# First unit of a retention and softplus FFN kernel: attention in chunk runs at five slots, and a new order of the weight conversions

## The chip, the cores and the metric

One core of one Trainium2 chip runs the whole program. The metric is device time in microseconds, the median of three runs. Five engines matter: PE (TensorE), DVE (VectorE), ACT (ScalarE), POOL (GpSimd) and SP, which issues all transfers. Each works through its own instructions in program order, and semaphores tie them together.

## The reference

Eight sequences of 576 tokens with eight heads of 64 go through a retention layer (scores times a decay matrix, no softmax). Its output, 4608 rows of 512, goes through a feed-forward layer with softplus between two products.

```python
scores = scale * np.matmul(q, k.transpose(0, 1, 3, 2))
Dmat = np.where(rel >= 0, gamma[:, None, None] ** rel[None, :, :], 0.0)
x = np.matmul(scores * Dmat, v)          # then heads side by side: (4608, 512)
...
h = x @ w_in                             # 512 -> 2048
g = np.maximum(h, 0.0) + np.log1p(np.exp(-np.abs(h)))
return g @ w_out                         # 2048 -> 512
```

The weights arrive as float64. The kernel makes float32 values of them on the chip, and splits every factor of the big products into a head and a rest, so that each product is three matmuls.

## The kernel before, in words

**Units and chunks.** The 4608 tokens are nine units of 512; a unit is four chunks of 128 tokens. The attention of a chunk is two steps (`m`), one for each half of the heads, so steps 2c and 2c+1 belong to chunk c. A step has scores (`scores_mm`, into `S`), sums for the running state (`sums_mm`, into `T`), and, once the scores are masked (`a`, DVE) and the states are there (`u` and `s` on DVE, `sx` and the decay of `s` on POOL), values and cross products (`values_mm`, `cross_mm`, into `O`). All of these are products of 64 x 64 tiles, four of which fill the array.

**The opening** (about the first 23 us) does chunks 0 to 3, the tokens of unit 0, with whole-tile forms, and converts the first weight pieces.

**The first unit** is the loop `for i in range(NF)` of 16 slots, and this is where the change lies. Slot i computes a block of `h` for unit 0 (12 matmuls, `hidden_mm`), its softplus (ACT: Abs, Exp, Ln; DVE: `softplus`; ACT: head `softplus_split`; DVE: rest `softplus_rest`), and the output product `y` of slot i-1 (12 matmuls, `output_some`). So `y` of slot i stands on PE behind `h` of slot i+1, and begins with the rest of `g`. Beside it each slot converts two weight pieces, one of w_in (`win`) and one of w_out (`wout`). A piece takes five steps: `weight_p` (ACT), `weight_t` (DVE), `weight_b` (DVE, needs p and t), `weight_c` (ACT, the head), `weight_d` (DVE, the rest). `weight_dl` is d, then the load of the piece five further on into the freed buffer `wst`, then for `win` the store to `split`. Meanwhile the attention of chunks 4 to 8 is needed for unit 1: every odd slot runs one step's scores and sums and the values of the step before, as three single runs on PE ahead of `h`.

**After it** come `plain_slot` calls, where a whole chunk is done in one run by `chunk_products(steps, done)`: scores and sums of a chunk, values and cross products of the chunk before it, interleaved by row groups of the array. In that run a one-element memset on POOL (`mark`) stands between the first sums and the second ones, since both row groups write one bank. The first such run, ahead of the first plain slot, takes the half chunk left over by the single steps; the second has one done step instead of two.

POOL scales the values of a step as soon as they are loaded (`scale_values`), decays the states, and makes the rest of the attention output `xt` (`half_x`).

Of the kernel before, what the change touches and what calls it, by code (L numbers as in the profile page):

```python
# [19 lines left out]
P = 128  # L20
# [20 lines left out]
START_WEIGHTS = 3  # L41
OPENING = 3
NOPEN = AHEAD + 2
# [3 lines left out]
NPIECE = 2 * NF  # L47
NJ = NF // 2
OPEN1 = 6
# [20 lines left out]
LAST = 320  # L70

# [13 lines left out]
def retention_softplus_ffn(ctx: ExitStack, tc, first, whole, others, consts, w, out):  # L85
# [6 lines left out]
    const, att, moe = pool("const", 1), pool("att", 2), pool("moe", 2)  # L92
    rawp, xpool, wpool = pool("rawp", 2), pool("xpool", 1), pool("wpool", 1)
# [8 lines left out]
    later = {}  # L102
# [47 lines left out]
    def load_rest(m):  # L150
        place = later["odd"] if m >= 2 * CHUNKS - 1 and m % 2 else rawp
# [7 lines left out]
    def load_step(m):  # L159

        if m == 0:
            at = 0
            for x in parts:
                nc.sync.dma_start(x, first[:, at:at + x.shape[1]])
                at += x.shape[1]
            k, q = parts[0][:, 0:2 * C], parts[0][:, 2 * C:4 * C]
            kp, v = parts[1][:, 0:2 * C], parts[1][:, 2 * C:4 * C]
        else:
            if m < NOPEN:
                place = openp if m < OPEN1 else openp2  # L170
                r = place.tile([P, 8 * C if m < FIRST else RAW], F32, name=f"raw{m}")
# [152 lines left out]
    def chunk_products(steps, done):  # L324
# [18 lines left out]
        for n in range(max(len(x) for x in pairs)):  # L343
            if n == 2 * len(steps) and sums_of(steps, 0):
                mark = nc.gpsimd.memset(later["mark"].tile([1, 1], F32, tag="mark", name="mark"), 0.0)
# [134 lines left out]
    def logs(h):  # L480

        ab = moe.tile([P, T], F32, tag="ab", name="ab", bufs=ABUFS)
        nc.scalar.activation(ab, h, AF.Abs)
        nc.scalar.activation(ab, ab, AF.Exp, scale=-1.0)
        nc.scalar.activation(ab, ab, AF.Ln, bias=1.0)
        return ab

# [73 lines left out]
    def load_weight(n):  # L561
        if n < NPIECE:
            wl[n] = wst.tile([P, PIECE, 2], I32, tag="wst", name="wst", bufs=WBUFS)
            nc.sync.dma_start(wl[n].rearrange("p c a -> p (c a)"), w[n // 2, n % 2])
# [24 lines left out]
    def weight_dst(n):  # L589
        p = n // 2  # L590
        if n % 2:
            return wouts[p][:, HI], wouts[p][:, LO]
# [13 lines left out]
    def weight_store(n):  # L606
        if n < NPIECE and n % 2 == 0:
            nc.sync.dma_start(split[n // 2].bitcast(F32), wins[n // 2].bitcast(F32))
# [88 lines left out]
    first_a, first_b = {3: 0, 5: 1, 6: 2}, {4: 0, 6: 1}  # L697
# [22 lines left out]
    def next_scores(m):  # L720
        new = ps_open.tile([P, 2, T], F32, tag="pair", name="pair")
        if m < FIRST:
            scores_whole(m, new)
        else:
            scores(m, new)
        return new
# [4 lines left out]
    for m in range(AHEAD):  # L731
        if m < FIRST:
            bank = (ps_att if m % 2 else ps_val).tile([P, 2, T], F32, tag="bank" if m % 2 else "val", name="bank")
            sums_whole(m, bank)
            values_whole(m, bank)
            if m == 0:
                next_scores(1)
            if m + 2 < AHEAD:
                new = next_scores(m + 2)
            ready = live[m]  # L740
            if m < FIRST - 1:
                state_whole(m, ready)
            if m == 0:
                scale_values(1)
            if m + 2 < AHEAD:
                scale_values(m + 2)
            parts_out = values_out(m, nc.gpsimd if m < FIRST - 1 else nc.vector)
            if m == 0:
                masked_whole(1)
            if m + 2 < FIRST:  # L750
                masked_whole(m + 2)
            if m == FIRST - 1:
                weight_b(2)
            parts_out()
            if m == FIRST - 1:
                weight_c(2)
            if m == FIRST - 1:
                scale_values(AHEAD)
                state_whole(m, ready)
        else:  # L760
            sums(m, new)
            scores_out(m)
            states_out(m)
        if m in first_a:
            weight_a(first_a[m])
        if m in first_b:
            weight_b(first_b[m])
            weight_c(first_b[m])
        if m == 5:
            weight_dl(0)  # L770
        if m == AHEAD - 1:
            weight_d(2)
        if m == AHEAD - 2:
            load_step(AHEAD + 1)
    weight_dl(1)
    load_weight(WBUFS + 2)
    weight_store(2)
# [5 lines left out]
    constant[0] = constants(consts_sb[:, 0:SMALL], consts_sb[:, SMALL:])  # L783


    for i in range(NF):
        n = START_WEIGHTS + 2 * i
        m = AHEAD + (i - 1) // 2
        step = i % 2
        if step:  # L790
            bank = ps_att.tile([P, 2, T], F32, tag="bank", name="bank")
            scores(m, bank)
            sums(m, bank)
            values(m - 1, bank)
# [5 lines left out]
        if i == 1:  # L800
            weight_dl(n - 1)
        weight_b(n)
        if i:
            weight_t(n + 1)
        h = hidden_mm(i, i % 2)
        ab = logs(h)
        if i > 1:
            weight_dl(n - 1)
        if i < NF - 1:
            softplus(h, ab)  # L810
        if i == 0:
            weight_t(n + 1)
        if step:
            _, t, cols = place(m - 1)
            where = (B11, B21)[(m - 1) % 2], STAGE[(m - 1) % 2, t], cols
            halves_out(m - 1)
            scores_out(m)
            states_out(m)
            if i < NF - 1:
                scale_values(m + 1)  # L820
            if m == NOPEN:
                open_pools.close()
                place_weights(ctx.enter_context(tc.tile_pool(name="wpool2", bufs=1)), NF)
        if i == NF - 1:
            softplus(h, ab)
        weight_c(n)
        if not step:
            weight_dl(n)
        gs[0, i] = softplus_split(ab)
        softplus_rest(gs[0, i], ab)  # L830
        if step:
            weight_dl(n)
            half_x(*where, nc.gpsimd)
        weight_p(n + 1)
        weight_b(n + 1)
        if n + 2 >= NPIECE and "ring" not in later:
            weight_pools.close()
            for name, bufs in (("ring", RING), ("odd", 2)):
                later[name] = ctx.enter_context(tc.tile_pool(name=name + "2", bufs=bufs))
            load_step(2 * CHUNKS - 1)  # L840
            scale_values(2 * CHUNKS - 1)
# [8 lines left out]
    for name, bufs in (("quad", QUADS), ("mark", 2), ("sum", 1)):  # L850
        later[name] = ctx.enter_context(tc.tile_pool(name=name + "2", bufs=bufs, side="right"))
    two = later["two"] = ps_att.tile([P, 2, T], F32, tag="bank", name="two")
# [4 lines left out]
    groups = [([m + 1], [m])]  # L857
    for ch in range(m // 2 + 1, NCHUNK + 1):
        groups.append(([2 * ch, 2 * ch + 1] if ch < NCHUNK else [], [k for k in (2 * ch - 2, 2 * ch - 1) if k > m]))
    groups = groups[::-1]  # L860

    def next_steps(steps):
        ks = [k for m in steps for k in ((m + 1, m + 2) if len(steps) == 1 else (m + 2,)) if k < NSTEP]
# [11 lines left out]

    def values_taken(steps, done):
        if steps:
            scores_out(*steps)
        if done:
            halves_out(*done)  # L880

    def group_out(steps, done):
        values_taken(steps, done)
        if steps:
            states_out(*steps)
# [12 lines left out]
    def plain_slot(u, p, xa, xb, rest, group=None, blocks=(), jobs=(), starts=()):  # L898
# [3 lines left out]
        ahead = u == 1 and p == 0  # L902
        if ahead:
            chunk_products(*group)
            coming_steps = next_steps(group[0])
# [7 lines left out]
        if ahead:  # L913
            group_out(*group)
        elif group:
# [5 lines left out]
        if group and not ahead:  # L921
# [78 lines left out]
    def store_out(j):  # L1000
# [3 lines left out]
        (0, prepare, PLAIN + 1), (0, prepare_whole, PLAIN), (0, prepare_sums, PLAIN), (1, prepare_split, PLAIN),  # L1004
# [450 lines left out]
```

## Time and profile before

| | |
|---|---|
| median of 3 runs | 817.8 us (817.5 to 818.37) |
| profiled execution, span | 815.8 us |
| PE busy | 808.2 us (99%) |
| DVE, ACT, POOL busy | 560.6, 389.2, 123.7 us |
| moved by DMA | 211.75 MB, mean 260 GB/s |
| granted TensorE clock | 0.9 or more in all 40 slices |

The profiled execution is 2.0 us shorter than the median, which counts what lies around the span. The page gives busy times, the chain of work that ended last (from the last instruction back to what released each step), and groups of instructions by line. TensorE's busy share alone says little here, since its instruction ends are modelled; the chain tells where it waited.

### The profile page before, as it was taken

How to read it: one execution, taken by the hardware profiler on the slowest of the kernel's cores; microseconds unless marked ns; L12 is line 12 of the kernel's file. 1: busy time of each engine (PE TensorE's matmuls, PEld its weight loads, DVE VectorE, ACT ScalarE, POOL GpSimd, SP SyncE). 2: the span in 40 equal slices, each digit the busy share in tenths (PEclk: the TensorE clock that was granted, in tenths of full speed). 3: DMA queues.
4: the chain of work that ended last, by engine and by line, in shares of the span. 5: the costliest groups of instructions: out<-in, count | busy, mean ns of one | idle time of the engine just before them, and what ended most of it. 6: DMA issues, size and time to landing. Idle time of an engine off the chain costs nothing.

```text
span 815.8 us, 18681 instructions
## 1 busy us (share of the span) xinstructions
PE 808.2 (99%) x7322; PEld 666.2 (82%) x7322; DVE 560.6 (69%) x953; ACT 389.2 (48%) x681; POOL 123.7 (15%) x223
## 2 busy tenths in 40 slices
PE   8999999999999999999999999999999999999998
PEld 6788888888888888888888888888888888888886
DVE  5999976777666774867669974555679944335785
ACT  6888863334323244434344554324355734434553
POOL 4322321320321420112122001112100000000000
PEclk9999999999999999999999999999999999999999
DMA  9998979989899882798987777878657776666674
GB/s 359 324 318 292 313 239 389 334 312 324 264 311 359 304 315 79 239 330 271 310 286 236 220 229 244 261 235 264 215 177 217 221 246 193 196 191 194 194 221 159
DMA packets 149847, 211.75 MB, mean 260 GB/s; under 512 B 10880, under 2 KB 114816, under 8 KB 149760
## 3 DMA queue, kind: packets, MB, share of 16 engines
q1 hardware_dynamic: 149760, 210.56, 78.3%
q8 instruction: 59, 0.97, 0.5%
q14 instruction: 28, 0.23, 0.1%
HBM read 168.05 MB, written 42.47 MB: 258 GB/s over the span
## 4 chain that ended last, share of the span: by engine, by line
PE 95%; DMA 2%; DVE 2%; ACT 0%; issue 0%; SPq 0%; DVEq 0%
PE acc L892 22%; PE sum L1183 20%; PE y L518 16%; PE two L892 14%; PE h L475 5%; PE two L1183 4%; PE third L892 3%; PE third L211 2%; PE third L1183 2%; PE acc L1183 2%; PE two L195 2%; PE two L299 2%; PE two L311 1%; DMA raw<-others 1%; DMA raw<-whole 1%; DVE wst L587 0%
## 5 line engine op out<-in xcount | busy, mean ns | idle before, releaser
L892 PE MATMUL acc<-xt,ring 128*128 128x512 f32 x780 | 196.4, 389 | 0.1
L892 PEld LDWEIGHTS acc<-xt,ring 128*128 128x128 f32 x780 | 146.3, 188 | 30.9 <-issue 0.3
L1183 PE MATMUL sum<-parts,ring 128*128 128x512 f32 x708 | 170.9, 392 | 0.0
L1183 PEld LDWEIGHTS sum<-parts,ring 128*128 128x128 f32 x708 | 131.6, 188 | 27.8
L1177 DVE TENSOR_TENSOR parts<-g,parts 128x512 fp32r<-128x512 f32 x168 | 115.4, 694 | 45.0 <-ACT parts L1173 42.3
L518 PE MATMUL y<-wout,g 128*128 128x512 f32 x564 | 137.2, 392 | 0.3 <-DVE g L497 0.3
L1173 ACT CAST parts<-g 128x512 fp32r<-128x512 f32 x168 | 103.9, 622 | 67.6 <-DVE parts L1177 27.3
L518 PEld LDWEIGHTS y<-wout,g 128*128 128x128 f32 x564 | 104.8, 188 | 22.9 <-DVE g L497 0.7
L892 PE MATMUL two<-xt,ring 128*128 128x512 f32 x486 | 123.3, 389 | 0.0
L892 PEld LDWEIGHTS two<-xt,ring 128*128 128x128 f32 x486 | 91.2, 188 | 18.9
L1205 ACT ACTIVATE g<-g 128x512 f32<-128x512 f32 x72 | 45.3, 629 | 59.4 <-DVE g L1220 35.6
L188 POOL TENSOR_TENSOR qv<-qv,consts_sb 128x256 f32<-128x256 f32 x61 | 47.4, 778 | 164.7 <-DMA qv<-others 157.7
L1220 DVE TENSOR_TENSOR g<-two,g 128x512 f32<-128x512 f32 x24 | 16.6, 692 | 77.8 <-PE two L892 77.8
L1218 ACT COPY g<-acc 128x512 f32<-128x512 f32 x24 | 14.1, 588 | 77.6 <-PE acc L892 77.6
L497 DVE TENSOR_TENSOR g<-ab,g 128x512 fp32r<-128x512 f32 x42 | 32.3, 769 | 26.4 <-ACT g L493 25.7
L493 ACT CAST g<-ab 128x512 fp32r<-128x512 f32 x42 | 26.1, 621 | 46.2 <-PE y L518 41.5
L475 PE MATMUL h<-xt,win 128*128 128x512 f32 x192 | 47.4, 396 | 0.3 <-DVE win L604 0.3
L475 PEld LDWEIGHTS h<-xt,win 128*128 128x128 f32 x192 | 35.3, 188 | 8.2 <-DVE win L604 0.6
L1258 ACT ACTIVATE g<-acc 128x512 f32<-128x512 f32 x24 | 14.3, 598 | 49.3 <-PE acc L892 49.3
L211 PEld LDWEIGHTS third<-qv,keys 64*64 64x64 f32 x776 | 27.0, 134 | 8.9 <-issue 7.7
L253 DVE TENSOR_TENSOR a<-two,mask 128x512 f32<-128x512 f32 (+1 forms) x28 | 19.0, 679 | 22.2 <-PE third L211 15.2
L1183 PE MATMUL two<-parts,ring 128*128 128x512 f32 x144 | 33.6, 389 | 0.0
(177 smaller groups left out, 1190.4 us busy)
## 6 DMA issues: line engine op xcount, KB each, us to landing
ring<-split SPq DMA_DIRECT2D x121, 256.0 KB, 4.9
ring<-combined SPq DMA_DIRECT2D x108, 256.0 KB, 3.9
ring<-outcombined SPq DMA_DIRECT2D x96, 256.0 KB, 3.5
qv<-others SPq DMA_DIRECT2D x61, 320.0 KB, 5.5
ring<-outsplit SPq DMA_DIRECT2D x72, 256.0 KB, 3.8
wst<-w SPq DMA_DIRECT2D x32, 512.0 KB, 5.8
keys<-others SPq DMA_DIRECT2D x61, 256.0 KB, 5.4
split<-win SPq DMA_DIRECT2D x16, 512.0 KB, 6.7
```

What stands on the lines that cost most here:

```text
L188: nc.gpsimd.tensor_mul(v, v, f.unsqueeze(2).broadcast_to([P, 4, D]))
L211: mm = nc.tensor.matmul(L["T"][rows[h], t, part[s]], L["kp"][rows[t], s, rows[h]], L["v"][rows[t], s, rows[h]], start=True, stop=True, ski ...
L253: nc.vector.tensor_mul(a[:, :, at], src.rearrange("p h (s c) -> p h s c", c=HC), mask.unsqueeze(1).unsqueeze(1).broadcast_to([P, 2, 2 * le ...
L475: nc.tensor.matmul(h, wins[p][:, a, kt * P:(kt + 1) * P], xt[:, b, T1 + half, kt % 2], start=(n == 0), stop=(n == 3 * NKT - 1))
L493: nc.scalar.copy(g[:, HI], ab)
L497: nc.vector.tensor_sub(g[:, LO], ab, g[:, HI].bitcast(F32))
L518: nc.tensor.matmul(ys[u][tt], g[:, a, tt * P:(tt + 1) * P], wouts[p][:, b], start=(p == 0 and n == 0), stop=(p == NF - 1 and n == 2))
L892: nc.tensor.matmul(bank, w[:, ta, kt * P:(kt + 1) * P], xt[:, tb, x, kt], start=start and k == 0, stop=k == 5, skip_group_check=True)
L1173: nc.scalar.copy(t[:, HI], g_slot(J, n))
L1177: nc.vector.tensor_sub(t[:, LO], g_slot(J, n), t[:, HI].bitcast(F32))
L1183: nc.tensor.matmul(bank[m], w[:, a, m * P:(m + 1) * P], t[:, b], start=start and n == 0, stop=n == 2, skip_group_check=True)
L1205: nc.scalar.activation(c, c, AF.Softplus)
```

## The change

The attention of chunks 4 to 8 moves from single steps at the odd slots to whole-chunk runs at slots 1, 4, 8, 12 and 15 (`GROUPS`), placed on PE behind `h` of the slot rather than ahead of it. Step 8 leaves the opening. The run writes its sums to the other `h` bank (`third`). Steps 8 to 13 use four rotating buffers; loads and scalings are placed by tables (`LOADS`, `SCALES`). The weight pieces are converted in a new order (`PIECES`: win of slot i+1 ahead of wout of slot i), with the five steps of a piece at new places between the softplus steps. The run ahead of the first plain slot is gone, the one two slots later is a whole one, and the last `y` of the unit comes ahead of the first plain slot.

```diff
-START_WEIGHTS = 3
-NOPEN = AHEAD + 2
+STEPS1 = 14
+PIECES = [(0, 0)] + [x for i in range(NF - 1) for x in ((i + 1, 0), (i, 1))] + [(NF - 1, 1)]
-OPEN1 = 6
+OPEN1 = 7
...
+GROUPS = {1: (4, None), 4: (5, 4), 8: (6, 5), 12: (7, 6), 15: (8, 7)}
+ODD = 12
+LOADS = {4: (12, 13), 8: (14, 15), 12: (16, 17), 15: (18, 19)}
+SCALES = {2: (10, 11), 7: (12, 13), 11: (14, 15), 14: (16, 17)}
...
-        if m >= AHEAD:
+        if m >= FIRST:
             nc.gpsimd.tensor_mul(v, v, f.unsqueeze(2).broadcast_to([P, 4, D]))
...
-    first_a, first_b = {3: 0, 5: 1, 6: 2}, {4: 0, 6: 1}
+    first_a, first_b = {3: 0, 5: 1, 6: 2}, {4: 0, 6: 1, 7: 2}
...
-    for m in range(AHEAD):
+    for m in range(FIRST):
...
     for i in range(NF):
-        n = START_WEIGHTS + 2 * i
-        m = AHEAD + (i - 1) // 2
-        step = i % 2
-        if step:
-            bank = ps_att.tile([P, 2, T], F32, tag="bank", name="bank")
-            scores(m, bank)
-            sums(m, bank)
-            values(m - 1, bank)
-            if i < NF - 1 and m + 1 >= NOPEN:
-                load_step(m + 1)
-        weight_p(n)
-        weight_t(n)
-        weight_c(n - 1)
...
+        near, out_now, far, out_next = 2 * i + 1, min(2 * i + 2, NPIECE - 1), 2 * i + 3, 2 * i + 4
...
+        group = [chunk_steps(ch) for ch in GROUPS.get(i, ())]
         h = hidden_mm(i, i % 2)
-        ab = logs(h)
...
+        if group:
+            later["third"] = ps_h.tile([P, T], F32, tag=f"h{(i + 1) % 2}", name="third")
+            chunk_products(*group)
...
+            for k in LOADS.get(i, ()):
+                load_step(k)
+        ab = moe.tile([P, T], F32, tag="ab", name="ab", bufs=ABUFS)
+        nc.scalar.activation(ab, h, AF.Abs)
+        weight_dl(near)
+        weight_t(far)
+        weight_c(out_now)
+        weight_dl(out_now)
+        weight_t(out_next)
+        nc.scalar.activation(ab, ab, AF.Exp, scale=-1.0)
+        weight_p(far)
+        if group:
+            states_out(*group[0])
+        weight_b(far)
+        nc.scalar.activation(ab, ab, AF.Ln, bias=1.0)
+        weight_p(out_next)
+        softplus(h, ab)
+        weight_b(out_next)
         gs[0, i] = softplus_split(ab)
         softplus_rest(gs[0, i], ab)
+        weight_c(far)
+        if group:
+            values_taken(*group)
+            for m in group[1]:
+                _, t, cols = place(m)
+                half_x((B11, B21)[m % 2], STAGE[m % 2, t], cols, nc.gpsimd)
+        for k in SCALES.get(i, ()):
+            scale_values(k)
...
+    output_some(CPU)
     for p in range(2 * PLAIN):
-        group = groups.pop() if p % 2 == 0 else None
+        group = groups.pop() if p and p % 2 == 0 else None
```

On PE a slot pair before is `h`, `y`, then a step as three runs with a new `bank`, then the next `h`; L195 are scores, L211 sums, L299 values, L311 cross products. Slot 5 of before:

```order
L518 MATMUL y_668<-wout_182,g 128x512 x3
L195 MATMUL bank<-qv,keys 64x64 x8
L211 MATMUL bank<-qv,keys 64x64 x8
L299 MATMUL bank<-a,raw_530 64x64 x8
L311 MATMUL bank<-raw_530,s 64x64
...
L311 MATMUL bank<-raw_530,u 64x64
L475 MATMUL h<-xt,win_828 128x512 x12
```

The chunk run of slot 4 in the changed kernel, its middle and its end; L203 are scores, L307 values, L319 cross products, L219 sums:

```order
L203 MATMUL two<-raw 64x64
L307 MATMUL two<-a,raw 64x64
...
L307 MATMUL two<-a,raw 64x64 x9
L319 MATMUL two<-raw,s 64x64
L219 MATMUL third<-raw 64x64
...
L319 MATMUL two<-raw,sx 64x64
L219 MATMUL third<-raw 64x64
L518 MATMUL y_657<-wout_185,g 128x512 x3
```

The attention now stands between `h` and `y`, at fewer places, and its sums go to `third`, the bank of the next `h`.

On ACT, L483 to L485 (before) and L801, L807, L812 (changed) are Abs, Exp and Ln, L574 is `weight_p`, L599 `weight_c`, L493 the head of `g`. A slot before:

```order
L483 ACTIVATE ab<-h 128x512
L484 ACTIVATE ab<-ab 128x512
L485 ACTIVATE ab<-ab 128x512
L599 CAST wout_184<-wst 128x512
L493 CAST g<-ab 128x512
L574 ACTIVATE wst<-wst 128x512 x2
L599 CAST win_914<-wst 128x512
```

The same in the changed kernel:

```order
L801 ACTIVATE ab<-h 128x512
L599 CAST wout_187<-wst 128x512
L807 ACTIVATE ab<-ab 128x512
L574 ACTIVATE wst<-wst 128x512
L812 ACTIVATE ab<-ab 128x512
L574 ACTIVATE wst<-wst 128x512
L493 CAST g<-ab 128x512
L599 CAST win_935<-wst 128x512
```

A weight step now stands between each two softplus steps, and Ln comes two instructions later.

On POOL, L452 is the rest of `xt`, L196 the scaling of a step's values, L282 and L289 the copies of `sx`, L301 the decay of `s`. Around the run of slot 8 the changed kernel has:

```order
L353 MEMSET mark 1x8
L282 COPY sx<-s 64x256
L289 COPY sx<-u 64x256
L301 TENSOR_TENSOR s<-s,consts_sb 128x256
L452 TENSOR_TENSOR xt<-xs,xt 128x2x128 x2
L196 TENSOR_TENSOR qv<-qv,consts_sb 128x256 x2
L353 MEMSET mark 1x8
```

Before, each odd slot had one `xt` and one scaling; now two and two follow each other directly behind a run, with nothing between them on POOL.

## Rows read from the trace of the kernel before

**Rows 1.** Page, part 1, and two stretches (length, engine busy, clock, DMA share, GB/s)

```profile
PE 808.2 (99%) x7322; PEld 666.2 (82%) x7322; DVE 560.6 (69%) x953; ACT 389.2 (48%) x681; POOL 123.7 (15%) x223
...
20.00:40.00 20.00, 18.74 (x218) 14.57 (x213) 18.96 (x36) 16.28 (x32) 7.87 (x12) 1.00 0.95 337
40.00:60.00 20.00, 20.00 (x146) 16.42 (x147) 18.29 (x35) 17.11 (x30) 4.46 (x8) 1.00 0.90 306
```

**Rows 2.** Chain, 48 to 53 us: start, length, engine, tile, line, count

```profile
48.48 2.72 PE y L518 x12
51.20 0.39 PE bank L195 x16
...
52.29 2.95 PE h L475 x12
```

**Rows 3.** Chain, from the end of the first unit to the third chunk run

```profile
118.95 0.07 issue
...
120.17 2.96 PE acc L892 x12
...
134.02 0.20 PE third L211
...
135.57 2.95 PE y L518 x12
...
159.82 0.20 PE third L211
...
161.84 2.95 PE y L518 x12
```

**Rows 4.** PE in order of time: start, length, line, tile, in brackets idle before

```profile
20.88 0.46 PE L195 MATMUL pair<-raw 64*64 64x64 f32 x16 [0.64 <-DMA raw<-others]
...
22.90 3.01 PE L475 MATMUL h<-xt,win 128*128 128x512 f32 x12
...
26.77 3.03 PE L475 MATMUL h<-xt,win 128*128 128x512 f32 x12
...
35.55 3.02 PE L518 MATMUL y<-wout,g 128*128 128x512 f32 x12 [0.28 <-DVE g L497]
...
40.00 3.04 PE L475 MATMUL h<-xt,win 128*128 128x512 f32 x12 [0.35 <-DVE win L604]
```

**Rows 5.** DVE in order of time, end of the opening and slots 3 to 4

```profile
23.80 0.87 DVE L417 TENSOR_TENSOR xt<-x,xt 128x256 fp32r<-128x256 f32 x1
...
25.32 0.68 DVE L604 TENSOR_TENSOR win<-wst,win 128x512 fp32r<-128x512 f32 x1
25.92 0.78 DVE L604 TENSOR_TENSOR wout<-wst,wout 128x512 fp32r<-128x512 f32 x1
...
49.50 0.92 DVE L587 SCALAR_TENSOR_TENSOR wst<-wst 128x512 int32<-128x512 int32 x1
50.34 0.96 DVE L581 TENSOR_SCALAR wst<-wst 128x512 int32<-128x512 uint32 x1
```

**Rows 6.** ACT in order of time, the softplus of slot 3

```profile
43.14 0.60 ACT L483 ACTIVATE ab<-h 128x512 f32<-128x512 f32 x1
43.77 0.64 ACT L484 ACTIVATE ab<-ab 128x512 f32<-128x512 f32 x1
44.44 0.63 ACT L485 ACTIVATE ab<-ab 128x512 f32<-128x512 f32 x1
44.98 0.64 ACT L599 CAST wout<-wst 128x512 fp32r<-128x512 f32 x1
```

**Rows 7.** POOL in order of time, end of the opening and slots 3 to 4

```profile
23.77 0.62 POOL L188 TENSOR_TENSOR raw<-raw,part 128x256 f32<-128x256 f32 x1 [0.55 <-DMA raw<-others]
...
49.03 0.84 POOL L188 TENSOR_TENSOR qv<-qv,consts_sb 128x256 f32<-128x256 f32 x1 [1.12 <-DMA qv<-others]
49.83 1.19 POOL L444 TENSOR_TENSOR xt<-xs,xt 128x256 fp32r<-128x256 f32 x1
```

**Rows 8.** Tile wst, from the issue of a load to its landing

```profile
DMA to landing us min/median/max: 3.5/5.8/11.4
```

More of the change, by code (lines that the diff above doesn't have):

```diff
@@ L150, in load_rest @@
     def load_rest(m):
-        place = later["odd"] if m >= 2 * CHUNKS - 1 and m % 2 else rawp
+        place = rawp if m // 2 % 2 else later["odd"]
         qv = place.tile([P, RAW - KEYS], F32, tag="qv", name="qv")
@@ L606, in weight_store @@
     def weight_store(n):
-        if n < NPIECE and n % 2 == 0:
-            nc.sync.dma_start(split[n // 2].bitcast(F32), wins[n // 2].bitcast(F32))
+        p, second = PIECES[n]
+        if not second:
+            nc.sync.dma_start(split[p].bitcast(F32), wins[p].bitcast(F32))
     def weight_dl(n):
@@ L720, in next_scores @@
     def next_scores(m):
[L721 to L726, printed above, removed]
+        scores_whole(m, ps_open.tile([P, 2, T], F32, tag="pair", name="pair"))
     next_scores(0)
@@ L730, in retention_softplus_ffn @@
     masked_whole(0)
-    for m in range(AHEAD):
[L732 to L763, printed above, removed]
+    for m in range(FIRST):
+        bank = (ps_att if m % 2 else ps_val).tile([P, 2, T], F32, tag="bank" if m % 2 else "val", name="bank")
+        sums_whole(m, bank)
+        values_whole(m, bank)
+        if m == 0:
+            next_scores(1)
+        if m + 2 < FIRST:
+            next_scores(m + 2)
+        ready = live[m]
+        if m < FIRST - 1:
+            state_whole(m, ready)
+        if m == 0:
+            scale_values(1)
+        if m + 2 < AHEAD:
+            scale_values(m + 2)
+        parts_out = values_out(m, nc.gpsimd if m < FIRST - 1 else nc.vector)
+        if m == 0:
+            masked_whole(1)
+        if m + 2 < FIRST:
+            masked_whole(m + 2)
+        parts_out()
+        if m == FIRST - 1:
+            scale_values(AHEAD)
+            state_whole(m, ready)
         if m in first_a:
@@ new lines, in retention_softplus_ffn, with values_taken, group_out, chunk_steps @@
+    place_weights(ctx.enter_context(tc.tile_pool(name="wpool2", bufs=1)), NF)
+    two = later["two"] = ps_att.tile([P, 2, T], F32, tag="bank", name="two")
+    load_step(AHEAD + 2)
+    def values_taken(steps, done):
+        if steps:
+            scores_out(*steps)
+        if done:
+            halves_out(*done)
+    def group_out(steps, done):
+        values_taken(steps, done)
+        if steps:
+            states_out(*steps)
+    def chunk_steps(ch):
+        return [] if ch is None else [2 * ch, 2 * ch + 1]
@@ L837, in retention_softplus_ffn @@
+        if i >= NF - 2 and "ring" not in later:
             weight_pools.close()
[L838 to L841, printed above, removed]
+            later["ring"] = ctx.enter_context(tc.tile_pool(name="ring2", bufs=RING))
             for _ in range(RING):
@@ L849, in retention_softplus_ffn @@
     piece_pools.close()
-    for name, bufs in (("quad", QUADS), ("mark", 2), ("sum", 1)):
+    for name, bufs in (("quad", QUADS), ("sum", 1)):
         later[name] = ctx.enter_context(tc.tile_pool(name=name + "2", bufs=bufs, side="right"))
-    two = later["two"] = ps_att.tile([P, 2, T], F32, tag="bank", name="two")
     acc = ps_h.tile([P, T], F32, tag="h0", name="acc")
     later["third"] = ps_h.tile([P, T], F32, tag="h1", name="third")
-    groups = [([m + 1], [m])]
-    for ch in range(m // 2 + 1, NCHUNK + 1):
-        groups.append(([2 * ch, 2 * ch + 1] if ch < NCHUNK else [], [k for k in (2 * ch - 2, 2 * ch - 1) if k > m]))
+    groups = [(chunk_steps(ch) if ch < NCHUNK else [], chunk_steps(ch - 1)) for ch in range(CHUNKS, NCHUNK + 1)]
     groups = groups[::-1]
     def next_steps(steps):
-        ks = [k for m in steps for k in ((m + 1, m + 2) if len(steps) == 1 else (m + 2,)) if k < NSTEP]
+        ks = [m + 2 for m in steps if m + 2 < NSTEP]
         for k in ks:
@@ L912, in plain_slot @@
         ab = softplus_of(bank)
[L913 to L915 removed]
+        if group:
             chunk_products(*group)
@@ L920, in plain_slot @@
         gs[u, p] = softplus_split(ab)
-        if group and not ahead:
+        if group:
             values_taken(*group)
```

90 lines of the change are left out of this document (22 added, 68 removed).

## Prediction

> **What bounds the kernel now.** I read the page's busy times first, then the chain of work that ended last, then the engines in order of time from 18 to 62 us, where the change lies. PE is busy 808.2 of 815.8 us. Between 20 and 40 us it lacks 1.26 us, from 40 to 60 us nothing [rows 1]. The granted clock is 1.00 in both stretches, so every matmul here runs at the 2.4 GHz level and no term below is a clock term. From 40.00 us to the end of the first unit the chain is PE alone: `h` 2.72, `y` 2.72, a step, and so on [rows 2]. What the change can win is PE's own attention time and the few idle pieces before 40 us; what it can lose is that some `y` or `h` starts to wait for DVE, which is busy 18.3 of 20 us there [rows 1].
>
> **PE, attention.** A step costs 52.29 - 51.20 = 1.09 us, and the matmul row behind it is 2.95 instead of 2.72, 0.23 more for the switch back to the full array: 1.32 [rows 2]. Two steps, a chunk, are 2.64. A whole chunk run is 161.84 - 159.82 = 2.02 plus the same 0.23, or 2.25; a run with only half of the values is 135.57 - 134.02 = 1.55 [rows 3]. So a chunk gets 0.39 us cheaper, not more: the matmuls stay, and what goes is one switch and one slow start.
>
> Count from `h` of slot 3 (40.00 us) to the first plain product. Before: six steps, 6 x 1.32 = 7.92, and the half run with its wait and switch, 120.17 - 118.95 + 0.24 = 1.46 [rows 3]; together 9.4. After: four runs at slots 4, 8, 12, 15. Two are whole, 2.02. The one at 4 lacks half of the cross products, the one at 15 half of the sums; I put both at 1.8, between 1.55 and 2.02. With four switches this is 2 x 2.02 + 2 x 1.8 + 0.92 = 8.6. The run of the third plain slot becomes whole, + 0.47. Together 9.1, so **0.3 us less**.
>
> **The opening.** Before, PE waits 0.64 us at 20.88 for the data of step 8, starts `h` of slot 0 at 22.90 and of slot 1 at 26.77; later it idles 0.28 and 0.35 us on DVE, and reaches `h` of slot 3 at 40.00 [rows 4]. After, step 8 is gone from the opening, so `h` of slot 0 starts some 0.8 us earlier but then waits inside for the attention output of the last opening step (DVE, 23.80 + 0.87 [rows 5]). `h` of slot 1 then needs the rest of win 1, which ends at 26.00 before [rows 5]. In the new order it stands behind the xt rest, a state add and a `weight_b`, 24.67 + 0.2 + 0.6 + 0.7, about 26; the mask and copy of step 8 that stood there are gone. So slot 1 starts at 26.0, not 26.77. From there PE has `h` 2.72, the run of chunk 4 alone, `y` 2.72, `h` 2.72, `y` 2.72. That first run has no values; between a step's 1.09 and 1.55 I take 1.1, plus 0.23. `h` of slot 3 would start at 26.0 + 10.88 + 1.33 = 38.2: **1.8 us less**. (The first run's sums need the bank of `h` of slot 0, free when DVE has read it. I find that read ending at 28.8, the run's sums at 29.2, so it costs nothing; with DVE 1 us later, 0.6.)
>
> Against this stands **0.5 us** at `y` of slot 1. ACT reaches Abs of slot 1 about 1.4 us late, since it has the head of `g` and a `weight_c` of slot 0 ahead of it. Step 11's data (590 KB) now goes into the transfer queue at about 22 us, ahead of weight piece 6, whose `weight_t` stands in DVE's way; at 337 GB/s [rows 1] that is 1.7 us in the queue, of which I expect 0.6 to be seen. Bounds 0 and 1.2.
>
> **The chain of a slot.** Let T be the end of `h`. Two slots in a row without a run give `y` of a slot the due time T + 5.44 (`y` before it, `h` after it, 2.72 each). ACT starts an independent instruction 0.54 us after the one ahead (44.44 to 44.98) and Abs 0.10 after T (`h` 40.00 + 3.04, Abs 43.14) [rows 4, 6]. DVE's pitch is 0.60 (25.32 to 25.92) [rows 5]; a hand-over between engines I put at 0.05. Abs T + 0.10, c 0.64, Exp 1.18, p 1.72, Ln 2.29 to 2.92. On DVE `weight_b` starts at 2.44, `softplus` at 3.04, to 3.73. Head of `g` 3.78 to 4.40, rest 4.45 to 5.14, `y` at 5.20. Due at 5.44: a slack of **0.24 us** in slots 2, 5, 6, 9, 10 and 13. A slot with a run, and the slot ahead of it, have 2.25 more. The old order had Exp and Ln directly behind Abs and a softplus at 45.1, 2.0 after T, so this slack is thinner than before; nothing else of the reordering is worth time, as the counts of p, t, b, c and d stay.
>
> **POOL beside DVE.** Where POOL works on two tensors, DVE's own instructions stretch: `weight_b` at 49.50 took 0.92, `weight_t` at 50.34 took 0.96, while POOL had the scaling at 49.03 and `xt` at 49.83; the usual durations are 0.69 and 0.42. That is 0.23 to 0.54 for each POOL instruction [rows 5, 7]. Before, these fell in even slots, whose due time has a step (1.32) more. After, two `xt` and two scalings follow each other behind the runs of slots 4, 8 and 12. DVE is done with a run's slot some 0.8 us before the next T; the two `xt` fall from about T - 0.3 to T + 1.3, mostly into DVE's wait for the `weight_c` of that slot. The two scalings fall beside `weight_t`, `weight_b` or the rest in slots 5, 9 and 13, the three with the thin slack. 2 x 0.23 - 0.24 = 0.2 to 2 x 0.54 - 0.24 = 0.84 each; 0 if the data of the steps comes later than the rest of `g`. I take 0.4, nearer the low end because `weight_t` has the larger price and waits behind the other. Three times: **1.2 us**, bounds 0 and 2.5.
>
> The other waits: the POOL memset inside a run finds POOL idle, its earlier work ended a slot before; the sums' bank at slots 4 to 15 was read a slot before; the loads of 12, 13 and 16, 17 wait on SP for the run's end and hold up one weight load by about 2.7 us, which then lands about 0.5 us before its use. All nothing, with that cover.
>
> **Sum.** 815.8 - 0.3 - 1.8 + 0.5 + 1.2 = 815.4 us of span; with the 2.0 us between the span and the median of 817.8, **817.4 us**. From 130 us on the kernel is the same work on a full PE.
>
> **Rivals.**
> 1. No stall: the scalings miss the chain and piece 6 lands in time. Only PE's gain is left, -2.1: 815.7 us. For it: POOL's overlap before cost PE nothing in 80 us. Against it: the overlap stood in slots with slack. Chance 0.28.
> 2. POOL and DVE take turns: `xt` at 49.83 ends at 51.02 and the `weight_t` that started at 50.34 ends at 51.30, just one short run later, as though it had not begun [rows 5, 7]. Then each scaling holds a DVE instruction for its whole undisturbed 0.62 us [rows 7]: 2 x 0.62 - 0.24 = 1.0 in three slots, 3.0, and 0.8 at slot 1: -2.1 + 3.8 = +1.7, 819.5 us. For it: the ends that match. Against it: the first scaling can fall into DVE's wait. Chance 0.10. The Trainium skill, SBUF — State Buffer, section Who interferes with whom, has this as a rule: a DVE instruction with two SBUF inputs and a POOL instruction that reads SBUF lock each other out for a whole instruction. The ends in those rows agree with it, the 0.23 of the first does only in part, so the sum stays with the stretch seen.
> 3. Late weight loads, the slower side. The wout piece of a slot is loaded when the win piece of the slot before is done, T + 0.3, and wanted at T + 5.44 + 1.9: 7.0 us. Landing takes 3.5 to 11.4, median 5.8 [rows 8]. `weight_t` stands in order ahead of `weight_b`, `softplus` and the rest, so above 7.0 us each 0.1 is lost in every slot. The price passes the gain when landings average about 7.3 in 13 slots (3.9 us, 819.6). For it: DMA is 0.90 busy [rows 1] and bursts now hold two steps. Against it: the median leaves 1.2 us. Chance 0.10.
> 4. The run doesn't do what it says, as it waits for the bank in every one of five slots: only if DVE lags by a slot; inside the forecast's upper part.
>
> **How the numbers follow.** The forecast has 0.52, the rivals 0.28, 0.10 and 0.10. The forecast's own range is 816.2 to 818.9 (stalls from 0.5 to 3.2 against 2.1). The range for 8 in 10 goes to rival 1 with 0.4 to spare and to where rivals 2 and 3 begin: 815.3 to 819.5. About 0.2% (1.6 us) can be told from no change, so faster means under 816.2: rival 1 and a little, 0.30. Slower means over 819.4: half of rival 2, rival 3 and little else, 0.16. Same 0.54.
>
> **What would show it.** In the changed profile `h` of slot 3 should start at 38 to 39 us; runs should cost about 2.0; PE should show idle pieces of some 0.4 us ahead of `y` of slots 5, 9 and 13, ended by the rest of `g`, and none in 6 and 10. Idle in 2, 6 and 10 as well would mean that the slot's chain is longer than 5.2; idle on DVE ahead of `weight_t`, ended by a DMA, is rival 3. A first plain product later than 123 us would mean that the PE sum is wrong.

## The result, and the profile after

The changed kernel takes **830.5 us** (median of 4 runs, 829.3 to 831.3), the kernel before beside it 818.0. The ratio is 1.0148 [1.0130, 1.0167]: 1.5% slower, where 817.4 was predicted, with 815.3 to 819.5 as the range for 8 in 10. The profiled execution has a span of 828.3 us against 815.8, so 12.5 us have to be found, or 12.9 against the predicted span of 815.4.

The page's PE line and the two stretches of [rows 1], after the change:

```profile
PE 817.5 (99%) x7322; PEld 665.8 (80%) x7322; DVE 554.5 (67%) x935; ACT 384.2 (46%) x677; POOL 117.7 (14%) x214
...
20.00:40.00 20.00, 18.08 (x139) 13.21 (x139) 17.46 (x33) 14.54 (x28) 8.08 (x10) 1.00 0.92 350
40.00:60.00 20.00, 20.00 (x191) 16.44 (x191) 15.81 (x29) 15.01 (x28) 5.07 (x8) 1.00 0.83 288
```

The count of matmuls is the same, 7322, and PE is *busy* 9.3 us longer, at the same granted clock of 1.00. So most of the loss is no wait: the same matmuls take longer. Groups of PE instructions (count, busy us, mean ns, idle before), of the kernel before and then of the changed one:

```profile
L1183 PE MATMUL sum<-parts,ring 128*128 128x512 f32 x708 | 170.9, 392 | 0.0
L518 PE MATMUL y<-wout,g 128*128 128x512 f32 x564 | 137.2, 392 | 0.3 <-DVE g L497 0.3
L892 PE MATMUL two<-xt,ring 128*128 128x512 f32 x486 | 123.3, 389 | 0.0
L1183 PE MATMUL two<-parts,ring 128*128 128x512 f32 x144 | 33.6, 389 | 0.0
```

```profile
L1151 PE MATMUL sum<-parts,ring 128*128 128x512 f32 x708 | 175.1, 397 | 0.0
L518 PE MATMUL y<-wout,g 128*128 128x512 f32 x564 | 139.1, 396 | 1.9 <-DVE g L497 1.9
L865 PE MATMUL two<-xt,ring 128*128 128x512 f32 x486 | 123.3, 389 | 0.0
L1151 PE MATMUL two<-parts,ring 128*128 128x512 f32 x144 | 34.6, 395 | 0.0
```

Every group with `parts` or `g` as an operand is slower, the products of `xt` and `ring` hardly. (`ring` holds weight blocks that are read back from `split` and similar stores; `parts` are the head and rest of `g` in the later units, in tiles of the pool of `g` and in `quad` tiles by turns.) Counted from the end, matmul for matmul (the order there is the same in both), the changed kernel is behind by 2.8 us at the first plain product (125.61 us, against 120.11 and 2.72 for `y` of slot 15, which before still had to come: 122.83), 4.4 at 166 us, 5.2 at 322, 8.0 at 580 and 12.3 at the last one. So 7.9 us are lost in the last 660 us, where the work is the same as before.

The rest are waits. PE in order of time, the stretch of [rows 4]:

```profile
21.86 1.19 PE L483 MATMUL h<-xt,win 128*128 128x512 f32 x4
23.70 5.16 PE L483 MATMUL h<-xt,win 128*128 128x512 f32 x20 [0.65 <-POOL xt L425]
...
34.22 3.02 PE L483 MATMUL h<-xt,win 128*128 128x512 f32 x12 [1.06 <-DVE s L297]
37.44 3.02 PE L518 MATMUL y<-wout,g 128*128 128x512 f32 x12 [0.19 <-DVE g L497]
40.30 2.91 PE L483 MATMUL h<-xt,win 128*128 128x512 f32 x12
```

`h` of slot 2 waits 1.06 us for a DVE copy of the run's sums. The chain shows why that copy is late: it stands behind the `weight_t` of piece 6 (L581), whose load lands at 33.38.

```profile
25.82 7.56 DMA wst<-w
33.38 0.02 issue
33.41 0.04 DVE wst L581
33.44 0.30 issue
33.75 0.15 DVE s L297
```

Later `y` of slots 5, 9 and 13 wait, 0.39, 0.23 and 0.74, and then, in the plain slots, the `y` at 139.11 and the run at 150.28. PE's rows of these five (a matmul is recorded as 0.39 us long and the next one follows after 0.23, so a wait ahead of `y` costs 0.16 more than the idle time in the brackets):

```profile
62.31 0.97 PE L518 MATMUL y<-wout,g 128*128 128x512 f32 x3 [0.39 <-DVE g L497]
...
87.03 1.20 PE L518 MATMUL y<-wout,g 128*128 128x512 f32 x4 [0.23 <-DVE g L497]
...
112.26 0.97 PE L518 MATMUL y<-wout,g 128*128 128x512 f32 x3 [0.74 <-DVE g L497]
...
139.11 0.50 PE L518 MATMUL y<-wout,g 128*128 128x512 f32 x1 [0.39 <-DVE g L497]
...
151.17 0.27 PE L219 MATMUL third<-qv,keys 64*64 64x64 f32 x1 [0.43 <-POOL qv L196]
```

### The profile page after: what moved, and what is told of

It reads as the page before. It is cut to its first block, busy times and chain, and to the rows that moved or that the text cites. A ratio compares the mean times of both kernels' runs of the same rounds, so it can differ in the third digit from the quotient of the medians.

```text
span 828.3 us, 18638 instructions
## 1 busy us (share of the span) xinstructions
PE 817.5 (99%) x7322; PEld 665.8 (80%) x7322; DVE 554.5 (67%) x935; ACT 384.2 (46%) x677; POOL 117.7 (14%) x214
## 4 chain that ended last, share of the span: by engine, by line
PE 88%; DMA 7%; DVE 2%; ACT 1%; issue 1%; SPq 0%; POOL 0%; DVEq 0%
PE acc L865 21%; PE sum L1151 20%; PE y L518 13%; PE two L865 13%; PE two L1151 4%; PE h L483 3%; DMA wst<-w 3%; PE third L865 2%; PE third L219 2%; PE third L1151 2%; PE acc L1151 2%; DMA raw<-whole 2%; PE two L203 2%; PE two L307 2%; PE two L319 1%; DMA out<-quad 1%
## 5 line engine op out<-in xcount | busy, mean ns | idle before, releaser
L1151 PE MATMUL sum<-parts,ring 128*128 128x512 f32 x708 | 175.1, 397 | 0.0
L518 PE MATMUL y<-wout,g 128*128 128x512 f32 x564 | 139.1, 396 | 1.9 <-DVE g L497 1.9
L196 POOL TENSOR_TENSOR qv<-qv,consts_sb 128x256 f32<-128x256 f32 x58 | 44.5, 768 | 142.4 <-DMA qv<-others 142.2
L493 ACT CAST g<-ab 128x512 fp32r<-128x512 f32 x42 | 26.1, 622 | 52.2 <-PE y L518 41.7
L483 PE MATMUL h<-xt,win 128*128 128x512 f32 x192 | 47.2, 394 | 1.7 <-DVE s L297 1.1
L483 PEld LDWEIGHTS h<-xt,win 128*128 128x128 f32 x192 | 35.8, 188 | 10.8 <-DVE s L297 1.5
L261 DVE TENSOR_TENSOR a<-two,mask 128x512 f32<-128x512 f32 x32 | 22.0, 687 | 23.4 <-PE third L219 15.6
L219 PEld LDWEIGHTS third<-qv,keys 64*64 64x64 f32 x816 | 28.4, 134 | 9.8 <-issue 8.9
L219 PE MATMUL third<-qv,keys 64*64 64x64 f32 x816 | 34.3, 222 | 0.4 <-POOL qv L196 0.4
```

The costliest lines, as they stand in the source:

```text
L219: mm = nc.tensor.matmul(L["T"][rows[h], t, part[s]], L["kp"][rows[t], s, rows[h]], L["v"][rows[t], s, rows[h]], start=True, stop=True, ski ...
L261: nc.vector.tensor_mul(a[:, :, at], src.rearrange("p h (s c) -> p h s c", c=HC), mask.unsqueeze(1).unsqueeze(1).broadcast_to([P, 2, 2 * le ...
L483: nc.tensor.matmul(h, wins[p][:, a, kt * P:(kt + 1) * P], xt[:, b, T1 + half, kt % 2], start=(n == 0), stop=(n == 3 * NKT - 1))
L493: nc.scalar.copy(g[:, HI], ab)
L518: nc.tensor.matmul(ys[u][tt], g[:, a, tt * P:(tt + 1) * P], wouts[p][:, b], start=(p == 0 and n == 0), stop=(p == NF - 1 and n == 2))
L1151: nc.tensor.matmul(bank[m], w[:, a, m * P:(m + 1) * P], t[:, b], start=start and n == 0, stop=n == 2, skip_group_check=True)
```

## Experiment 1: where the operands lie

The diff also has a line that the excerpt above leaves out, `later = {"mark": pool("mark", 2)}`: it moves the pool of the marks from the end of the program to a place ahead of `rawp`. Its 64 B push `xt`, the wout parts, `xs` and the ring 64 B on; `g`, win and the quad tiles stay or move by 2048. In the compiled programs, all these tiles start at 192 modulo 256 before (`xt` 37312, ring 176576, `g` 19904, win 217024). After the change `xt`, wout and ring start at 0 modulo 256, `g`, win and quad still at 192. Each matmul has two operands in SBUF, its weights and its moving data, in this order: win and `xt` for `h`, `g` and wout for `y`, ring and `parts` for the sums, ring and `xt` for the products. Five kernels test whether these places are the cause, three of them the kernel *before* with a shift and nothing else.

```
after_pad    pool("mark", 2)  ->  pool("mark", 4)                     # 128 B in all
fit          pool("mark", 2)  ->  pool("mark", 16)                    # 512 B in all
before_s64   + pool("shift", 1).tile([P, 16], F32, name="shift")      # ahead of rawp
before_s256  + pool("shift", 1).tile([P, 64], F32, name="shift")
before_edge  edge.tile([P, 8], F32)  ->  edge.tile([P, 24], F32)      # moves win, quad
```

> The kernel before with nothing changed but an unused tile of 64 B ahead of xt, the wout parts, xs and the ring. Placement theory: it gets the changed kernel's slow matmuls with none of its new order: a sum matmul 233.3 ns, h and y blocks 2.75 us, and about 8.3 us more, 826. Rival (order or clock): unchanged, 818.0.

> The kernel before with nothing changed but an edge tile that is 64 B longer, which moves the right side of SBUF (the win parts, the converted weights, the quad tiles) by 64 B and leaves xt, wout, g and the ring. Placement theory, if it is the difference between the two operands that counts: h blocks (win against xt) go to 2.75 us, y blocks (g against wout) stay at 2.72, and those sums whose second operand lies in a quad tile become slow while those with parts in the pool of g stay at 226.7 ns; 3 to 5 us more, 821 to 823. If it is the place of xt, wout or the ring by itself that counts: unchanged, 818.0, as also by the rival (order or clock).

> The changed kernel with 64 more bytes reserved in the pool of the marks, so that everything allocated behind that pool (xt, the wout parts, xs, the ring) lies 64 B further on, at the same remainder by 128 as in the kernel before. Placement theory (a matmul is slower when its weights and its moving data lie at different remainders by 128 B): a sum matmul goes back from 233.3 to 226.7 ns, y and h blocks from 2.75 to 2.72 us, and the time falls by about 8.3 us, to 822. Rival, that the slower matmuls come from the new order of the work or from the clock: 230 ns and more stay, and the time stays at 830.5.

Measured: before_s64 826.5 us, ratio 1.0110 [1.0095, 1.0126]; before_edge 822.2, 1.0056 [1.0041, 1.0071]; both as the placement theory said. But after_pad gave 830.5, 1.0160 [1.0143, 1.0177], no gain. So placement costs, and the step of 128 was wrong. In after_pad the left tiles lie at 64 modulo 256, off by 128 from the others. The next two runs tried a step of 512, and then 256.

> The changed kernel with 448 more bytes in the pool of the marks, so that xt, the wout parts and the ring lie at the remainder by 512 that they have in the kernel before, the same as that of g, win and the quad tiles; nothing else is changed. Placement theory, as the runs with 64 and 128 B of difference leave it (a matmul is fast only where weights and moving data have the same remainder by 512): sums 226.7 to 227.5 ns, h and y blocks 2.72 us, and 8.3 us less than the changed kernel, about 822. Rival (the new order of the work slows the matmuls): still 229 ns and more, 830.5.

> The kernel before with nothing changed but an unused tile of 256 B ahead of xt, the wout parts, xs and the ring. It settles the step by which places repeat. If a remainder by 256 decides, nothing changes: 817.7. If it takes a remainder by 512, the left side is now off by 256 and the sums, y and h blocks are slow: 6 to 15 us more, 824 to 833.

Measured: fit 821.4, 1.0046 [1.0033, 1.0059]; before_s256 817.7, 1.0001 [0.9992, 1.0011]. 256 is the step among those tried. The sums of fit and of before_s256:

```profile
L1151 PE MATMUL sum<-parts,ring 128*128 128x512 f32 x708 | 170.9, 392 | 0.0
```

```profile
L1184 PE MATMUL sum<-parts,ring 128*128 128x512 f32 x708 | 170.9, 392 | 0.0
```

From the start of one 128x512 matmul to the next (means over rows between 200 and 260 ns), by the address of the moving data less that of the weights, modulo 256:

| kernel | h (177 to 181) | y (554, 555) | sums (985) | products (1344 to 1346) |
|---|---|---|---|---|
| before | 0: 228.3 | 0: 227.2 | 0: 227.1 | 0: 226.7 |
| after | 64: 229.1 | 64: 229.4 | 192: 233.3 | 0: 227.5 |
| before_s64 | 64: 229.5 | 64: 229.3 | 192: 233.3 | 0: 227.5 |
| after_pad | 128: 232.5 | 128: 232.5 | 128: 232.6 | 0: 227.9 |
| before_edge | 64: 229.7 | 0: 227.4 | half 0: 228.2, half 192: 233.2 | 0: 227.0 |
| fit | 0: 227.1 | 0: 227.6 | 0: 227.1 | 0: 226.7 |

It is the difference that counts, not the place: in before_edge, `h` slows down though `xt` stays where it was, and of the sums only those whose `parts` lie in a quad tile. The products become slower by 0.8 to 1.2 ns in three kernels although their own difference stays 0; why is open. After minus fit is (1.0148 - 1.0046) x 817.7 = **8.3 us**; from the table, 985 x 6.2 + 554 x 1.8 + 1345 x 0.8 + 177 x 2.0 ns = 8.5 us. And fit, which keeps the new order, is 5.8 us behind the kernel before at 166 us and 5.5 at the last matmul: behind the plain slots nothing is lost any more. (The trace of fit is the slowest of its five executions, 823.2 us against a median of 821.4.)

## Experiment 2: step 11's data and the late piece

```
LOADS = {1: (11,), 4: (12, 13), ...}      # on after_pad; load_step(AHEAD + 2) in the opening goes
```

> The changed kernel with the 64 more bytes, and step 11's data loaded behind the run of slot 1 instead of in the opening. Theory of the late piece (the weights of piece 6 land late behind step 11's data and hold up DVE, which reads the bank of the next h only afterwards): h of slot 2 loses its wait of 1.06 us and y of slot 1 its 0.19, and the time is 1.0 to 1.5 us below that of the changed kernel with the 64 bytes alone, about 820.7. Rival (the weights' landing of 7.6 us has another cause, the order of DVE alone): the wait of about 1 us ahead of h of slot 2 stays and the times of the two are equal.

Measured: 1.0158 [1.0143, 1.0173], against 1.0160 of after_pad, which is no difference in time. The pair can't decide between theory and rival, since `h` of slot 2 doesn't wait in after_pad at all: this wait changes from one execution to the next. All traces together can. In the five with step 11 in the opening, `y` of slot 1 waits 0.17 to 0.20 us (after, after_pad, fit, fit_sp, fit_ring), and `h` of slot 2 in three of them (1.06 in after, 0.43 in fit, 0.27 in fit_ring). In the five with step 11 moved (pad_l11, fit_all twice, fit_pool2, fit_early) neither waits. So the cause stands. Its price changes with the execution, and in the median it is too small to be seen here. Of the 0.53 us by which the first plain product starts earlier than in after_pad (124.51, 125.04), about 0.3 come from here and 0.2 from slot 13.

## Experiment 3: the queue of loads

```
fit_sp    - for k in LOADS.get(i, ()): load_step(k)          # behind chunk_products
          + the same two lines behind weight_dl(out_now)
fit_ring  + if i == NF - 2: weight_c(out_next); weight_dl(out_next)   # behind weight_c(far)
fit_all   both, and step 11 as above
```

> As the run fit, and the loads of steps 12 to 17 are issued behind the slot's two weight loads instead of ahead of them. Theory (SP waits for the run's end at those loads, and the weight load behind it lands too late): y of slots 5 and 13 lose most of their waits of 0.5 and 0.9 us, 1.0 to 1.4 us below fit, about 821. Rival (the waits come from POOL beside DVE): they stay, equal to fit within 0.3 us.

> As the run fit, and the last weight piece is finished at the end of slot 14 instead of in slot 15. Theory (the ring's tiles lie where that piece lies, so that SP's first ring load waits for it and all loads behind it come 3 to 5 us late): the ring loads start near 117 instead of 120 us, the wait ahead of the y at 139 us and the stretched run at 150 us go, and the time is 0.8 to 1.2 us below fit, about 821. Rival (these two waits have their cause in the loads of the plain part itself): equal to fit.

> As the run fit, with the edits of fit_sp and fit_ring and with step 11's data loaded behind the run of slot 1. If the three causes are separate their gains add: 822.2 less 1.2, 1.0 and 1.2, about 818.8, so still no faster than before at 817.8. What is then left against the 815.7 of the sum without any stall is the runs (0.4), the wait in h of slot 0 (0.8), that of slot 9 (0.4) and unknown pieces (1.5). Rival (the waits move on to the next slot): less than half of the sum is gained, 820.5 or more.

Measured on one chip with fit: fit_sp 1.0016 [1.0007, 1.0026], fit_ring 1.0022 [1.0013, 1.0031], fit_all 0.9999 [0.9990, 1.0008]. Times 817.7, that is 2.5, 2.0 and 3.8 us below fit, where up to 1.4, up to 1.2 and 3.4 were expected; the interval of fit alone is 1.1 us to either side, so the surplus isn't shown. What PE waited for from 40 to 170 us (us in total, times, longest), of fit, fit_sp and fit_ring (the traces are of 823.2, 818.5 and 820.3 us, so that of fit shows more than its median has):

```profile
PE y L518 <- DVE g L497: 3.5, 4, 1.6
PE third L219 <- POOL qv L196: 0.2, 1, 0.2
```

```profile
PE y L518 <- DVE g L497: 1.1, 1, 1.1
PE third L219 <- POOL qv L196: 0.5, 1, 0.5
```

```profile
PE y L518 <- DVE g L497: 1.5, 3, 0.9
```

In fit_sp the three waits at slots 5, 9 and 13 are gone, and the one left is in the plain slots; in fit_ring it is the other way round. The ring's theory holds. Of the queue's, the late load is in the chain of the changed kernel, ahead of `y` of slot 5:

```profile
51.66 7.53 DMA wst<-w
59.19 0.02 issue
59.21 0.04 DVE wst L581
...
61.56 0.70 DVE g L497
62.27 0.04 issue
62.31 0.73 PE y L518 x2
```

The weight load could have gone out when DVE had the win piece done, at 48.8. But SP's rows there are

```profile
50.58 1.00 SPq L180 DMA_DIRECT2D raw<-others  x2
51.66 0.38 SPq L564 DMA_DIRECT2D wst<-w  x1
```

It waits for the end of the run (50.65) with the loads of steps 12 and 13, and the weight load behind them goes out at 51.66, 2.9 us late. It lands 7.53 us later, `weight_t` takes it at once, and all behind that is late. At slot 13 it is the same, in each of the five traces with the old order of loads (after, after_pad, pad_l11, fit, fit_ring). But at slot 9 of all five, and at slot 5 of after_pad, pad_l11 and fit_ring, it is the rival (at slot 5 of fit, both). No load is late there; `weight_t` and `weight_b` take 0.83 and 1.10 us instead of 0.42 and 0.69, beside the two scalings on POOL. DVE and then POOL of the changed kernel at slot 9:

```profile
83.14 0.83 DVE L581 TENSOR_SCALAR wst<-wst 128x512 int32<-128x512 uint32 x1
83.89 1.10 DVE L587 SCALAR_TENSOR_TENSOR wst<-wst 128x512 int32<-128x512 int32 x1
```

```profile
82.63 1.82 POOL L196 TENSOR_TENSOR qv<-qv,consts_sb 128x256 f32<-128x256 f32 x2
```

fit_sp ends these waits too, because its loads of the steps, and so the scalings, come later: at slot 9 the first scaling starts 0.80 us behind `weight_t` and no longer 0.51 ahead of it. So the 2.5 us are for both causes together, and the time doesn't tell them apart. The ring's cause shows in the rows of the ring's loads between 110 and 128 us (first and last start), of before, after and fit_ring:

```profile
L636 SPq DMA_DIRECT2D ring<-split x10: 524/609/611, 114.6 to 126.2; - x10
```

```profile
L637 SPq DMA_DIRECT2D ring<-split x8: 594/610/617, 120.0 to 124.6; - x8
```

```profile
L637 SPq DMA_DIRECT2D ring<-split x8: 594/610/1407, 116.4 to 121.8; - x8
```

After the change the last weight piece is finished in slot 15, at 119.97, where DVE's rest of it ends. The ring's tiles wait for that. With the piece finished a slot earlier, the loads start at 116.4.

fit_all shows what the change is worth without these waits: no difference. It reaches the first plain product at 121.38, 1.4 us ahead of before (122.83), and is 0.4 ahead at 165 us. The single gains add up to 2.5 + 2.0 + 0.2 = 4.7, of which 3.8 are measured; with about 1 us of uncertainty on each, that is no more than a hint that some of it is lost again further on.

## Experiment 4: POOL, the opening, and where the gain goes

```
fit_pool2  in scale_values, for steps 12 to 17, ahead of the scaling:
           nc.gpsimd.tensor_mul(twice, v, f.unsqueeze(2).broadcast_to([P, 4, D]))
fit_early  scale_values(8) behind parts_out() of step 6; weight_dl(1) ahead of weight_b(2)
```

> As fit_all, with every scaling of steps 12 to 17 on POOL done twice, the first time into a tile that nobody reads. It prices the term POOL beside DVE. Theory (each POOL instruction beside a chain in slots 5, 9 and 13 costs 0.23 to 0.54 of DVE time): the wait of 0.3 ahead of y of slot 5 grows to 0.6 to 1.0 and waits of 0.3 to 0.6 appear ahead of y of slots 9 and 13: 1.0 to 2.0 us above fit_all. Rival (the overlap mostly hits DVE's own idle time): below 0.4 us.

> As fit_all, with two turns in the opening: the scaling of step 8 stands behind the xt part of the step ahead on POOL, and the rest of win 1 stands ahead of the next piece's bit step on DVE. Theory (h of slot 0 waits 0.8 us on POOL, and h of slot 1 then for DVE's win): h of slot 1 starts 0.4 to 0.8 us earlier and the time is 0.4 us below fit_all, about 817.1. Rival (y of slot 0 has no slack and takes over the wait): equal to fit_all. A second rival for all gains in the first unit: in the plain slots the loads of steps 20 and 21 land at 145.7 us whatever PE does, so that what is won ahead is lost in the run that waits for them.

> fit_all once more, beside fit_pool2 and fit_early on one chip: 817.5, equal to the kernel before within 0.2%.

Measured on one chip: fit_all_again 0.9991 [0.9982, 0.9999], fit_pool2 1.0001 [0.9992, 1.0011], fit_early 0.9987 [0.9978, 0.9995].

fit_pool2 has only one wait on this account in its trace, 0.20 us ahead of `y` of slot 5 (0.14 in fit_all), and none at slots 9 and 13. That fits the rival. But the trace is of its fastest execution, 816.7 us, and others took up to 820.3. Its ratio is 0.0010 above that of fit_all_again, 0.8 us, and the two intervals leave room for anything from nothing to about 2. So the theory's 1.0 to 2.0 isn't confirmed, and isn't excluded by the time either. How POOL and DVE meet is plain in the trace, though. DVE and then POOL in order of time:

```profile
57.82 1.03 DVE L590 SCALAR_TENSOR_TENSOR wst<-wst 128x512 int32<-128x512 int32 x1
58.78 1.10 DVE L500 TENSOR_TENSOR g<-ab,g 128x512 fp32r<-128x512 f32 x1
```

```profile
57.69 0.61 POOL L198 TENSOR_TENSOR twice<-raw,consts_sb 128x256 f32<-128x256 f32 x1 [2.01 <-DMA raw<-others]
58.38 0.94 POOL L199 TENSOR_TENSOR raw<-raw,consts_sb 128x256 f32<-128x256 f32 x1
59.29 1.06 POOL L198 TENSOR_TENSOR twice<-raw,consts_sb 128x256 f32<-128x256 f32 x1
```

The first POOL instruction ends at 58.30, and DVE's, begun at 57.82, at 58.85, 0.55 later; POOL's next ends at 59.32, 0.47 after that; DVE's at 59.88, 0.56 after that. Each end follows the other engine's by one short run, as in taking turns: rival 2's mechanism, which the Trainium skill has as an exclusive lock for the whole instruction (SBUF — State Buffer, section SBUF: two separate sides); the order of the ends agrees with it, but 0.47 to 0.56 is less than the undisturbed 0.61 (POOL) and 0.69 (DVE), so part of each instruction does run beside the other. The rule as the prediction has it is for two SBUF inputs; `weight_t`, with one, is stretched as well (0.83 instead of 0.42 at slot 9). Rival 2's price, 1.0 us in each of three slots, was too high: `y` is delayed in one slot of this trace, by 0.20 of idle time.

fit_early brings `h` of slot 1 to 3.22 us after `h` of slot 0, from 3.97 and 4.17 in the two runs of fit_all. 0.4 of that is lost at once, as the run of slot 1 then waits for DVE to have read the bank of `h` of slot 0. And `h` of slot 0 itself starts later, at 22.48 instead of 21.42 and 21.75, so that `h` of slot 1 comes at 25.70, between the 25.39 and 25.92 of the other two. It is the fastest kernel here, by 0.13% against before, but its interval overlaps that of fit_all_again, so that a gain over it isn't shown.

The gain in the first unit is cut by DMA. Of the 1.4 us that fit_all is ahead at the first plain product, 1.1 are left at 146 us and 0.4 behind the run there. In the four kernels that reach the first plain product at 121.4 to 121.8, the `y` behind the run at 146 us starts at nearly the same time:

| kernel | first plain product | run | `y` behind it | run takes |
|---|---|---|---|---|
| fit_all | 121.38 | 145.49 | 148.22 | 2.73 |
| fit_all_again | 121.48 | 145.59 | 148.03 | 2.44 |
| fit_pool2 | 121.57 | 145.68 | 147.91 | 2.23 |
| fit_early | 121.83 | 145.96 | 147.98 | 2.02 |

The run waits for the scaling of step 21, whose data lands at 145.7 in fit_all and at 145.5 and 145.4 in the next two; the earlier PE is there, the longer it waits. In fit_early the data lands at 144.8, and the run waits for nothing; so the landing isn't at 145.7 whatever PE does, as the expectation had it. In fit_all the transfers keep the 16 DMA engines full from 118 to 150 us (packets, MB, share of their time):

```profile
q1 hardware_dynamic: 7436, 11.72, 102.1%
```

That the loads themselves would go faster with less traffic there was not tried.

## Why the prediction was wrong, by its own steps

1. **"From 130 us on the kernel is the same work on a full PE."** The same work, but not at the same speed: 8.3 of the 12.9 us (the changed kernel against fit; the kernel before loses 8.9 by the 64 B alone). The step that failed isn't a term of the sum but one that was left out: this sentence puts everything behind 130 us at nothing. The move of the mark pool stood in the diff, and the prediction doesn't mention it. Durations were carried over from [rows 2, 3] as if they belonged to an instruction, while part of them belongs to the operands' addresses.
2. **"The other waits ... all nothing, with that cover": part of 2.5 us.** The hold-up behind the loads of the steps was seen and its length right (2.9, forecast 2.7). The cover wasn't: a landing of 5.8, the median of [rows 8], was set against it, and the two took 7.53 and 6.45. The first came 2.9 + 7.53 = 10.4 us after its due time, and with a run in the slot 7.0 + 2.25 = 9.25 were left. So it is rival 3, in slots 5 and 13: DVE idles 0.87 and 1.26 us ahead of `weight_t` there until the DMA lands, the sign that the prediction names for it, and `y` then 0.39 and 0.74. fit_sp gave 2.5 us, but took POOL's waits away with these.
3. **The ring's loads: 2.0 us.** The prediction follows the weight pieces to PE and not to the memory they give back. The last piece is converted by 119.97 instead of 114.18, 5.8 us later, where the kernel as a whole is some 3 us behind, and SP's queue behind the ring loads carries all loads of the plain slots.
4. **Attention, -0.3.** The runs are 2.02 long as forecast for whole ones, the ones at 4 and 15 too (48.63 to 50.65, 117.99 to 120.00), where 1.8 was put; that is 0.44 more, and nothing is left of the 0.3. The short run of slot 1 took 1.36 without the switch, put at 1.1; that is 0.26 more.
5. **The opening, -1.8 + 0.5.** In the changed kernel `h` of slot 3 starts at 40.30. With step 11 out of the way it is 38.33 in fit_all, and 38.2 was forecast, so the mechanism was right. That it is so close is partly luck: `h` of slot 1 started at 25.39 instead of 26.0, and from there it took 12.9 us instead of 12.2. Two terms were missed: the scaling of step 8 ahead of `xt` on POOL (0.65), and the sums' bank of the run in slot 1: the text asks when the run may write it, not when DVE has copied the sums out, for which `h` of slot 2 waits (1.06). The cause, piece 6 behind step 11, was in the text, with 0.6 at `y` of slot 1.
6. **POOL beside DVE, +1.2.** Mechanism and size hold where the scalings meet the chain. At slot 9 of the changed kernel they stretch DVE's work by 0.82, and `y` waits 0.23 of idle time, 0.39 in all, where 0.4 was put. At slots 5 and 13 the late loads stood in their place. With the loads of the steps moved, the scalings come later, and in fit_all 0.14 of idle time is left, at slot 5. So the forecast's three equal waits are one of this kind and two of another.

A first plain product past 123 us was to show that the PE sum was wrong. It came at 125.61, but the sum of PE's own work was short by 0.44 + 0.26 = 0.7 only (point 4); the rest was waits and slow matmuls.

## What to carry to other kernels

When a diff adds, moves or resizes a tile, write down the start addresses of the matmul operands before and after, and keep weights and moving data at the same remainder by 256 B; here an unused 64 B tile cost 8.9 us (826.5 against 817.6), more than all waits of the change together. A load that waits in a queue for a buffer holds up every load behind it, so issue it behind those that are due sooner, and ask for each pool which later pool lies on its memory. Price the wait behind a late load by the longest landing seen, not by the median.

## What the runs showed of the hardware

On this chip a 128x512 fp32r matmul followed the one before after 226.7 to 228.3 ns when moving data and weights started at the same remainder by 256 B, 229 to 230 at a difference of 64, 232.5 at 128 and 233.3 at 192, all at a granted clock of 1.00 (the 2.4 GHz level). A difference of 64 was measured on `h` and `y` alone and 192 on the sums alone, so what sets these two apart may also be the kind of block. Two kernels without any other change show it in time: 64 B, 1.0110 [1.0095, 1.0126]; 256 B, 1.0001 [0.9992, 1.0011]. Other sizes and types were not tried, nor where in the path the time goes.

The Trainium skill (SBUF — State Buffer, section A bandwidth-pool intuition that's wrong (but worth ruling out)) gives the weight load a second, independent read port. These runs differ: how the addresses of weights and moving data stand to each other changes the rate, by 0.5% (`h` of before_s64, 229.5 against 228.3) to 2.7% (sums, 233.3 against 227.1), with nothing else changed; the measurement decides.
